# Attention, expert and softplus kernel: score products on keys laid out as block diagonals, scores issued ahead of the previous tile's turning, two score banks, another order of early loads

## The chip, the cores and the metric

The kernel runs on one core of a Trainium2 chip. The metric is device time of the whole program in microseconds (us); a run's time is that of one execution, and the median of several runs is compared. Five engines work side by side and meet through semaphores: TensorE (PE; its weight loads are shown apart as PEld), VectorE (DVE), ScalarE (ACT), GpSimd (POOL) and SyncE (SP), which here issues most transfers. Each engine takes its own instructions strictly in the order in which they are queued. PSUM has 8 banks of 128 x 512 fp32.

## The reference, cut to what matters

```python
def _attn_ref(q, k, v):                      # B, H, S, D = 4, 8, 576, 64
    scores = np.matmul(q, k.transpose(0, 1, 3, 2)) / np.sqrt(D)
    rel = pos[:, None] - pos[None, :]
    mask_plain = (rel >= 0) & (rel < 32)                      # heads 0 to 3
    mask_dil = (rel >= 0) & (rel < 128) & (rel % 4 == 0)      # heads 4 to 7
    scores = np.where(masks, scores, -1e9)
    attn = np.exp(scores - scores.max(-1, keepdims=True))
    attn = attn / (attn.sum(-1, keepdims=True) + 1e-09)
    return np.matmul(attn, v)

def reference(...):
    x = attn_out.transpose(0, 2, 1, 3).reshape(2304, 512)
    x = _moe_ref(x, ...)     # each token to the one of 8 experts with the largest logit
    return _moe2_ref(x, ...) # softplus(x @ w_in) @ w_out
```

## The kernel before, in words

**Stages.** The program is one long list written out by hand. First come 20 attention tiles (4 batches of 5; tile `w` of batch `b` covers 128 query positions, the last of a batch 64), mixed with the routing of tokens to experts. Then the eight experts ("ranks", the largest expert known first as rank 0) follow, and then the softplus part in blocks of 384 tokens. PE, ACT, DVE and SP take their instructions in the order of the Python text (`manual_schedule`, L1020); pools (`bufs`) decide when a buffer is free again.

**Keys and queries.** `load_qk` (L258) brings 576 KB of q or k of four heads into a `raw` tile; `transpose_qk` (L295) turns 512 columns at a time on PE into a PSUM tile `pqk`, and `evict_qk` (L287) copies from there into `qT` (scaled, L291 on DVE or L293 on ACT) or `kT` (L289 on ACT). There are ten such units a batch (`QK_UNITS`), of which eight are turned by L304 and two small ones, with the ninth piece of both q and k, by L314. In `qT` and `kT` the 64 dimensions of one head lie on partitions 0 to 63, those of the other head of a pair on 64 to 127. Units of the next batch are spread over the tiles of this one by `QK_0` and `QK_AT` (tile by tile, how many; `some_qk`). `load_v` (L266) fills `vP` (heads 0 to 3) and `vD` (heads 4 to 7); `fills` (L235) writes zeros with GpSimd into the parts of them that must be empty.

**One tile.** `scores` (L338) first writes the mask into two PSUM banks with two products against an identity (L346), then adds 32 products of 64 partitions, 32 queries and 64 (or 48) keys (L361), 16 for each half of the partitions, each half into its own bank. `softmax` (L371) takes the minimum of each 64 (the scores carry a minus sign; L376, result `mx`) and subtracts (L377, result `p`) on DVE; `exps` (L383) is one exponential on ACT in place. `transpose_p` (L387) turns `p` on PE (L391, result `pp`), `evict_p` copies it out on ACT (L400, `pt`). `values` (L403) are 16 products of 128 partitions, 32 queries and 128 columns (L418, result `o`); `sums` (L422) and `normalise` (L433) on DVE make the row sums (L426 to L430) and `x` (L440), which SP stores to DRAM (L447, L450). `transpose_x` turns x on PE (L457, `px`), `evict_x` copies it on ACT (L468, `xT`).

**Routing.** For each of six groups of tiles `logits_of` makes router products (L478, `pl`); the generators `logits`, `route` and `pick` add small DVE steps (`lt`, L494 and L497; turned on PE at L500; one-hot `roh`, L551; rank products on PE at L564 to L568). `pump` takes the next one or two of these steps at fixed places in a tile's text, so they stand between the softmax and normalising steps. `events` places single steps of the end by tile number: at tile 18 the first expert weights are split on ACT (L759, `wh`) and DVE (L704, `wl`).

**The order in a step.** The loop at L1101 runs `i` from 0 to 21. A step issues, in this order: turning and copying of p of tile i-1, scores of tile i, the step's turnings of q and k but one, turning of x of tile i-2, softmax and exponential of tile i, values, sums and normalising of tile i-1, the last turning of q and k. So the scores of a tile stand behind the turning of the previous tile's p on PE, and there is one pair of score banks (`ps_s`, `bufs=1`).

**Start.** SP's queue begins with q and k of batch 0, then v's plain half (`load_v(0, 0)`), q and k of batch 1's first half, v's dilated half (`load_v(0, 1)`); L1021 to L1033.

Of the kernel before, what the change touches and what calls it, by code (L numbers as in the profile page):

```python
# [40 lines left out]
def attn_moe_softplus_kernel(ctx: ExitStack, tc: tile.TileContext, q, k, v, w_gate, w_ogate, w1, w2, w_in, w_out, out, dbg=None):  # L41
# [177 lines left out]
    ps_s = psctx.enter_context(tc.tile_pool(name="ps_s", bufs=1, space=PSUM))  # L219
# [5 lines left out]

    SH = 8
    QS = S + 64 + SH
    qT = [per_p[i].tile([P, 2, 2, QS], F32, name=f"qT{i}") for i in range(2)]  # L230
    kT = [per_p[i].tile([P, 2, 2, S + SH], F32, name=f"kT{i}") for i in range(2)]
# [3 lines left out]
    def fills(i):  # L235


        for h2 in range(2):
            nc.gpsimd.memset(qT[i][64 * h2 : 64 * h2 + 64, 1, :, S + SH * h2 :], 0.0)
# [55 lines left out]
    def transpose_qk(b, half, ti, y):  # L295
# [3 lines left out]
        ps = ps_t.tile([P, 512], F32, tag="tp", name=f"pqk{b}{half}{ti}{y}")  # L299
        if y < 2:  # L300
# [4 lines left out]
            for o in range(2):  # L305
                src = ps[64 * o : 64 * o + 64].rearrange("q (j x p) -> q x p j", j=4, x=2)
                dst = (qT, kT)[ti][b % 2][64 * y : 64 * y + 64, half, :, SH * y : SH * y + S]
                dst = dst.rearrange("q x (p j) -> q x p j", j=9)[:, :, :, y + o : y + o + 7 : 2]
                evict_qk(b, half, ti, dst, src)
        else:  # L310
# [27 lines left out]
    def scores(b, w):  # L338

        i = b % 2  # L340
        s = ps_s.tile([P, 2, 512], F32, tag="s", name=f"s{b}{w}")
        mask = mask_w[:, 0:1].to_broadcast([P, 4, 64]) if w else mask_0.unsqueeze(2).to_broadcast([P, 2, 2, 64])
        for h2 in range(2):
            o = s[:, h2, :256]
            o = o.rearrange("q (c k) -> q c k", k=64) if w else o.rearrange("q (a c k) -> q a c k", a=2, k=64)
            nc.tensor.matmul(o, identb, mask, start=True, stop=False, skip_group_check=True)  # L346
        for half in range(2):
            nk = 64 if w < 4 or half == 0 else 48
            for hp in range(2):
                for u in range(4):  # L350
                    for h2 in range(2):
                        rows = slice(64 * h2, 64 * h2 + 64)
                        q_, k_ = [t[rows, half, hp, SH * h2 : SH * h2 + n_] for t, n_ in ((qT[i], S + 64), (kT[i], S))]
                        if half == 0:
                            n = 4 * w + (u if w < 4 else u % 2)
                            q0, k0 = 32 * n, 32 * max(n - 1, 0)
                        else:
                            q_, k_ = [t.rearrange("q (m r) -> q r m", r=4)[:, u] for t in (q_, k_)]
                            q0, k0 = 32 * w, 32 * max(w - 1, 0)
                        c = 64 * (2 * half + hp)  # L360
                        nc.tensor.matmul(  # L361
                            s[32 * u : 32 * u + 32, h2, c : c + nk],
                            q_[:, q0 : q0 + 32],
                            k_[:, k0 : k0 + nk],
                            start=False,
                            stop=(half == 1 and hp == 1 and u == 3),
                            skip_group_check=True,
                        )
        tl[b, w] = dict(s=s)

    def softmax(b, w):  # L371
        d = tl[b, w]
        mx = sm_p.tile([P, 2, 4], F32, tag="mx", name=f"mx{b}{w}")
        p = at_p.tile([P, 4, 2, 64], F32, tag="p", name=f"p{b}{w}")
        s = d["s"][:, :, :256].rearrange("q h (c k) -> q h c k", k=64)
        nc.vector.tensor_reduce(mx, s, AX.X, ALU.min)  # L376
        nc.vector.tensor_tensor(  # L377
            p.rearrange("q c h k -> q h c k"), mx.unsqueeze(3).to_broadcast([P, 2, 4, 64]), s, ALU.subtract
        )
        pump()  # L380
        d["p"] = p
# [513 lines left out]
    def acc(c):  # L895
        if ("a", c // 2) not in xacc:
            xacc["a", c // 2] = (ps_s, ps_o)[c // 2].tile([P, 2, 512], F32, tag="so"[c // 2], name=f"xacc{c}")
        xacc[c] = xacc["a", c // 2][:, c % 2]
# [127 lines left out]
    fills(0)  # L1026
    load_qk(1, 0)
    load_v(0, 1)
# [14 lines left out]
    QK_0 = [1, 2, 2, 2, 3]  # L1043
# [57 lines left out]
    for i in range(n + 2):  # L1101
# [13 lines left out]
        if 1 <= i < n + 1:  # L1115
            transpose_p(*tiles[i - 1])
            evict_p(*tiles[i - 1])
        if i < n:
# [12 lines left out]
            scores(b, w)  # L1131
        events(i, 0)
        some_qk(nqk - 1)
        if 2 <= i:
# [335 lines left out]
```

## Time and profile before

| what | us |
|---|---|
| median of 3 runs | 847.83 (847.11 to 848.87) |
| the profiled execution | 845.49 |
| its span, first to last instruction | 843.9 |
| attention tiles, first mask product to the end of the last scores | 15.1 to 148 |
| rest of routing, rank 0's tokens | to 179.8 |
| experts and softplus | 179.8 to 843.9 |
| PE busy over the span | 780.8 (93%) |
| DVE, ACT, POOL busy | 544.6, 470.6, 191.3 |

Times in the rows are us from the span's start, durations of one instruction ns where a "mean" stands. A group of instructions has one row: line, engine, operation, what is written and read, shape, count; then busy time and mean, and behind the second bar the time in which its engine sat idle just before it, with what ended most of that time ("issue": nothing that the profile shows). Products in fp32 leave two records each. PEclk is the mean granted share of TensorE's full clock.

### The profile page before, as it was taken

The page shows a single profiled execution, that of the slowest core. Times are in us where ns is not written, and L with a number is a line of the kernel's source. Part 1 is how long each engine was busy: PE and PEld are TensorE (multiplying, and loading weights), DVE is VectorE, ACT ScalarE, POOL GpSimd, SP SyncE. Part 2 cuts the span into 40 slices and gives each one's busy share as a digit, 9 for nine tenths or more (in the row PEclk, how much of TensorE's full clock was granted, in tenths as well). Part 3 has the DMA queues.
Part 4 walks back from the last instruction along what each step waited for, and adds up shares of the span by engine and source line. Part 5 has one row for each costly group of instructions (what it writes and reads, how often), then busy time and mean ns, then how long its engine had stood idle before and what let it go on. Part 6 is the DMA issues. An engine that isn't in the chain of part 4 may idle for free.

```text
span 843.9 us, 16072 instructions
## 1 busy us (share of the span) xinstructions
PE 780.8 (93%) x6202; PEld 705.4 (84%) x6203; DVE 544.6 (65%) x1074; ACT 470.6 (56%) x901; POOL 191.3 (23%) x171
## 2 busy tenths in 40 slices
PE   5788865799999999999799999999999999999995
PEld 4566644689899999999798888899999999999994
DVE  4467756473266767743679989886666665766653
ACT  3564533345456566655666666665655655655553
POOL 9101024325233533543201221211001001001001
PEclk8898989699999999999999999999999999999999
DMA  9959766317588889776841313231000001000000
GB/s 218 243 148 182 153 114 202 107 34 226 177 279 253 279 280 295 245 217 200 307 120 50 101 51 94 57 94 38 19 1 37 1 1 38 1 1 38 1 1 37
DMA packets 88850, 104.26 MB, mean 124 GB/s; under 512 B 31005, under 2 KB 65181, under 8 KB 88769
## 3 DMA queue, kind: packets, MB, share of 16 engines
q1 hardware_dynamic: 78688, 87.50, 37.5%
q0 software_dynamic: 3888, 10.12, 3.7%
q10 hardware_dynamic: 6192, 5.56, 2.0%
q8 instruction: 50, 0.82, 0.4%
q14 instruction: 32, 0.25, 0.1%
HBM read 83.98 MB, written 19.32 MB: 122 GB/s over the span
## 4 chain that ended last, share of the span: by engine, by line
PE 44%; issue 16%; DVE 7%; ACT 3%; POOL 1%; DMA 1%; SPq 0%; POOLq 0%; DVEq 0%
PE q L1379 4%; PE pg L843 4%; PE pg L844 4%; PE pg L842 4%; PE q L1377 4%; PE q L1378 4%; PE ph L842 3%; PE ph L844 3%; PE py L842 3%; PE ph L843 3%; PE py L843 3%; PE py L844 3%; DVE l L1357 1%; ACT gh L1363 1%; DVE l L1355 1%
## 5 line engine op out<-in xcount | busy, mean ns | idle before, releaser
L704 POOL TENSOR_TENSOR wl<-wr,wh 128x1024 fp32r<-128x1024 f32 (+1 forms) x46 | 98.2, 2144 | 207.6 <-ACT wh L788 108.2
L843 PE MATMUL pg<-xlm,wh 128*128 128x384 f32 x384 | 129.6, 338 | 0.0
L842 PE MATMUL pg<-xhm,wh 128*128 128x384 f32 x384 | 129.4, 337 | 0.0
L844 PE MATMUL pg<-xhm,wl 128*128 128x384 f32 x384 | 129.4, 337 | 0.0
L1379 PE MATMUL q<-wh,gl 128*128 128x512 f32 x288 | 114.1, 396 | 2.2 <-DVE gl L704 2.1
L1377 PE MATMUL q<-wh,gh 128*128 128x512 f32 x288 | 113.9, 396 | 0.5
L1378 PE MATMUL q<-wl,gh 128*128 128x512 f32 x288 | 113.0, 392 | 0.0
L1363 ACT CAST gh<-l 128x384 fp32r<-128x384 f32 x96 | 49.2, 512 | 99.7 <-DVE l L1357 99.7
L842 PE MATMUL ph<-xh,wh 128*128 128x424 f32 (+7 forms) x256 | 80.7, 315 | 3.9 <-DVE hl L856 2.3
L704 DVE TENSOR_TENSOR gl<-l,gh 128x384 fp32r<-128x384 f32 x96 | 57.1, 594 | 41.0 <-ACT gh L1363 38.1
L759 ACT CAST wh<-wr 128x1024 fp32r<-128x1024 f32 x72 | 75.2, 1048 | 14.5 <-ACT y L865 6.1
L843 PE MATMUL py<-hl,wh 128*128 128x424 f32 (+7 forms) x256 | 80.2, 313 | 2.4 <-DVE hl L856 2.4
L842 PE MATMUL py<-hh,wh 128*128 128x424 f32 (+7 forms) x256 | 81.3, 318 | 0.0
L1386 POOL DMA_INDIRECT out_dram<-o,perm_sb x18 | 18.6, 1034 | 271.9 <-DVE o L254 137.5
L844 PE MATMUL ph<-xh,wl 128*128 128x424 f32 (+7 forms) x256 | 80.1, 313 | 0.0
L844 PE MATMUL py<-hh,wl 128*128 128x424 f32 (+7 forms) x256 | 80.0, 312 | 0.0
L843 PE MATMUL ph<-xl,wh 128*128 128x424 f32 (+7 forms) x256 | 79.9, 312 | 0.0
L842 PEld LDWEIGHTS pg<-xhm,wh 128*128 128x128 f32 x384 | 72.1, 188 | 3.9
L843 PEld LDWEIGHTS pg<-xlm,wh 128*128 128x128 f32 x384 | 72.0, 188 | 3.9
L704 DVE TENSOR_TENSOR wl<-wr,wh 128x1024 fp32r<-128x1024 f32 x42 | 59.4, 1417 | 20.7 <-ACT wh L759 20.7
L844 PEld LDWEIGHTS pg<-xhm,wl 128*128 128x128 f32 x384 | 72.1, 188 | 0.0
L1348 DVE TENSOR_SCALAR w<-u 128x384 f32<-128x384 f32 x96 | 34.7, 361 | 56.5 <-ACT u L1346 55.7
(192 smaller groups left out, 1639.4 us busy)
## 6 DMA issues: line engine op xcount, KB each, us to landing
wr<-in_moe_w_dram SPq DMA_DIRECT2D x64, 512.0 KB
raw<-in_q_dram SPq DMA_DIRECT2D x8, 576.0 KB
raw<-in_k_dram SPq DMA_DIRECT2D x8, 576.0 KB
x2r<-yT_dram SPq DMA_DIRECT2D x12, 384.0 KB
vP<-in_v_dram SPq DMA_DIRECT2D x16, 272.0 KB
praw<-in_moe_w_in_dram SPq DMA_DIRECT2D x8, 512.0 KB
praw<-in_moe_w_out_dram SPq DMA_DIRECT2D x8, 512.0 KB
wr<-in_moe_w_in_dram SPq DMA_DIRECT2D x8, 512.0 KB
```

The lines of the kernel that those rows point to most:

```text
L704: e.tensor_tensor(lo, src, hi.bitcast(F32), ALU.subtract)
L759: (eng or nc.scalar.copy)(d[1], d[0])
L842: nc.tensor.matmul(ps, wh, xh, start=(first and i == 0), stop=False)
L843: nc.tensor.matmul(ps, wh, xl, start=False, stop=False)
L844: nc.tensor.matmul(ps, wl, xh, start=False, stop=(last and i == k - 1))
L1348: nc.vector.tensor_scalar(w_, u, 1.0, None, ALU.add)
L1355: nc.vector.tensor_tensor(l, l, w_, ALU.add)
L1363: nc.scalar.copy(gT[b, f][0], l)
L1377: nc.tensor.matmul(acc[b, t], gh[:, ts_], wh, start=(f == 0), stop=False)
L1378: nc.tensor.matmul(acc[b, t], gh[:, ts_], wl, start=False, stop=False)
L1379: nc.tensor.matmul(acc[b, t], gl[:, ts_], wh, start=False, stop=(f == NF - 1))
L1386: sc = nc.gpsimd.indirect_dma_start(out=out, out_offset=IndirectOffsetOnAxis(ap=perm_sb[:, b * (BT // P) + t, 0:1], axis=0), in_=o, in_off ...
```

## The change

What it does:

- **Keys as block diagonals.** `kT` gets one more dimension of two: for each half of the partitions only its own head's slot is filled and the other slot is zero (GpSimd, in `fills`). A product over all 128 partitions with two slots of 64 columns gives both heads' scores next to each other. `scores` issues 16 such products a tile and one mask product of 512 columns, all into one bank. The offset `SH` of the second head is gone, and with it the copies that covered all 128 partitions: the small copies of a pair (L317) are now made in two halves.
- **Two tiles' scores are held.** `ps_s` has two buffers of one bank.
- **Order in a step.** Scores and softmax come first, then turning and copying of p of the tile before; the exponential follows the first turnings of q and k; the sums of the tile before stand ahead of its values; one turning of q and k moves ahead of the values.
- **Early loads.** `load_v(0, 1)` goes ahead of `load_qk(1, 0)`; batch 1 is turned 0, 1, 3, 3, 3 units a tile (`QK_0`) in place of 1, 2, 2, 2, 3.
- **Buffers.** `p` and `pt` have two buffers in place of three, `x` five in place of six.

```diff
-    ps_s = psctx.enter_context(tc.tile_pool(name="ps_s", bufs=1, space=PSUM))
+    ps_s = psctx.enter_context(tc.tile_pool(name="ps_s", bufs=2, space=PSUM))
...
-    kT = [per_p[i].tile([P, 2, 2, S + SH], F32, name=f"kT{i}") for i in range(2)]
+    kT = [per_p[i].tile([P, 2, 2, 2, S], F32, name=f"kT{i}") for i in range(2)]
...
         for h2 in range(2):
-            nc.gpsimd.memset(qT[i][64 * h2 : 64 * h2 + 64, 1, :, S + SH * h2 :], 0.0)
+            nc.gpsimd.memset(kT[i][64 * h2 : 64 * h2 + 64, :, :, 1 - h2], 0.0)
+        nc.gpsimd.memset(qT[i][:, 1, :, S:], 0.0)
...
-            for t in range(2):
-                dst = (qT, kT)[t][b % 2][:, half, :, SH : SH + S].rearrange("q x (p j) -> q x p j", j=9)[:, :, :, 0]
-                evict_qk(b, half, t, dst, ps[:, P * t : P * t + P].rearrange("q (x p) -> q x p", x=2))
+            for y in range(2):
+                for t in range(2):
+                    src = ps[64 * y : 64 * y + 64, P * t : P * t + P].rearrange("q (x p) -> q x p", x=2)
+                    evict_qk(b, half, t, to(t, y)[:, :, :, 8 - 8 * y], src)
...
     def scores(b, w):
...
-        s = ps_s.tile([P, 2, 512], F32, tag="s", name=f"s{b}{w}")
...
-        for h2 in range(2):
-            o = s[:, h2, :256]
...
-            nc.tensor.matmul(o, identb, mask, start=True, stop=False, skip_group_check=True)
+        s = ps_s.tile([P, 512], F32, tag="s", name=f"s{b}{w}")
+        s4 = s.rearrange("q (c h k) -> q c h k", h=2, k=64)
...
+        nc.tensor.matmul(o, identb, mask, start=True, stop=False, skip_group_check=True)
...
-                    for h2 in range(2):
...
-                        nc.tensor.matmul(
-                            s[32 * u : 32 * u + 32, h2, c : c + nk],
-                            q_[:, q0 : q0 + 32],
-                            k_[:, k0 : k0 + nk],
...
+                    nc.tensor.matmul(
+                        s4[32 * u : 32 * u + 32, 2 * half + hp, :, :nk],
+                        qu[:, q0 : q0 + 32],
+                        ku[:, :, k0 : k0 + nk],
...
-        p = at_p.tile([P, 4, 2, 64], F32, tag="p", name=f"p{b}{w}")
+        p = at_p.tile([P, 4, 2, 64], F32, tag="p", name=f"p{b}{w}", bufs=2)
...
-        pt = at_p.tile([P, 4, P], F32, tag="pt", name=f"pt{b}{w}")
+        pt = at_p.tile([P, 4, P], F32, tag="pt", name=f"pt{b}{w}", bufs=2)
...
-        x = at_p.tile([P, 2, 4, D], F32, tag="x", name=f"x{b}{w}", bufs=6)
+        x = at_p.tile([P, 2, 4, D], F32, tag="x", name=f"x{b}{w}", bufs=5)
...
     load_v(0, 0)
     fills(0)
+    load_v(0, 1)
     load_qk(1, 0)
-    load_v(0, 1)
...
-    QK_0 = [1, 2, 2, 2, 3]
+    QK_0 = [0, 1, 3, 3, 3]
...
-        if 1 <= i < n + 1:
-            transpose_p(*tiles[i - 1])
-            evict_p(*tiles[i - 1])
...
             scores(b, w)
+            softmax(b, w)
+        if 1 <= i < n + 1:
+            transpose_p(*tiles[i - 1])
+            evict_p(*tiles[i - 1])
         events(i, 0)
         some_qk(nqk - 1)
+        if i < n:
+            exps(*tiles[i])
         if 2 <= i:
             transpose_x(*tiles[i - 2])
             evict_x(i - 2)
             pump()
         events(i, 1)
-        if i < n:
-            softmax(*tiles[i])
-            exps(*tiles[i])
+        if 1 <= i < n + 1:
+            sums(*tiles[i - 1])
         events(i, 2)
+        some_qk(min(nqk, 1))
         if 1 <= i < n + 1:
             values(*tiles[i - 1])
-            sums(*tiles[i - 1])
             normalise(*tiles[i - 1])
         events(i, 3)
-        some_qk(min(nqk, 1))
```

Three places in the queues show the move. A row names the line, the operation, what it writes and reads, and how many stand in a row; s is a tile's scores, pqk a turning of q or k, pp and px turnings of p and x, o the values (vP and vD the two halves of v). The weight load of the identity ahead of each mask product, and the second of two mask products alike, are not shown. PE's queue from the first tile's mask, before:

```order
L346 MATMUL s_327<-mask_86,identb 128x256
L361 MATMUL s_327<-kT_116,qT_114 32x64 x32
L304 MATMUL pqk_367<-identf,raw_222 128x128 x4
L391 MATMUL pp_374<-identf,p_363 128x128 x4
L346 MATMUL s_385<-mask_w,identb 128x256
L361 MATMUL s_385<-kT_116,qT_114 32x64 x32
L304 MATMUL pqk_420<-identf,raw_224 128x128 x4
L418 MATMUL o_432<-vP_118,pt_379 32x2x64 x8
L418 MATMUL o_432<-vD_120,pt_379 32x2x64 x8
```

and now:

```order
L346 MATMUL s_333<-mask_86,identb 128x512
L359 MATMUL s_333<-kT_116,qT_114 32x128 x16
L346 MATMUL s_360<-mask_w,identb 128x512
L359 MATMUL s_360<-kT_116,qT_114 32x128 x16
L388 MATMUL pp_382<-identf,p_352 128x128 x4
L306 MATMUL pqk_395<-identf,raw_231 128x128 x4
L415 MATMUL o_402<-vP_118,pt_387 32x2x64 x8
L415 MATMUL o_402<-vD_120,pt_387 32x2x64 x8
```

The scores of tiles 0 and 1 now run back to back and the turning of tile 0's p behind both; the first turning of batch 1's q has moved from ahead of that p to behind it, one step later; 32 products of 64 columns are 16 of 128.

PE's queue around the scores of tile 19, the last (px is tile 17's x and then tile 18's, pl the router products and plt the turning of the logits lt of one group of tiles), before:

```order
L457 MATMUL px_2374<-identf,x_2323 128x128 x4
L418 MATMUL o_2401<-vP_119,pt_2337 32x2x64 x8
L418 MATMUL o_2401<-vD_121,pt_2337 32x2x64 x8
L478 MATMUL pl_2425<-xT_2169,wg 32x128 x12
L500 MATMUL plt_2451<-identf,lt_2438 128x96
L391 MATMUL pp_2453<-identf,p_2387 128x128 x4
L346 MATMUL s_2460<-mask_w,identb 128x256
L361 MATMUL s_2460<-kT_117,qT_115 32x64 x16
L361 MATMUL s_2460<-kT_117,qT_115 32x48 x16
L457 MATMUL px_2495<-identf,x_2423 128x128 x4
```

and now:

```order
L454 MATMUL px_2074<-identf,x_2035 128x128 x4
L415 MATMUL o_2101<-vP_119,pt_2071 32x2x64 x8
L415 MATMUL o_2101<-vD_121,pt_2071 32x2x64 x8
L475 MATMUL pl_2125<-xT_1903,wg 32x128 x12
L346 MATMUL s_2146<-mask_w,identb 128x512
L359 MATMUL s_2146<-kT_117,qT_115 32x128 x8
L359 MATMUL s_2146<-kT_117,qT_115 32x2x48 x8
L497 MATMUL plt_2168<-identf,lt_2138 128x96
L388 MATMUL pp_2170<-identf,p_2063 128x128 x4
L454 MATMUL px_2178<-identf,x_2118 128x128 x4
```

Tile 19's mask and scores have moved ahead of the turnings of lt and of tile 18's p, behind which they stood.

DVE's queue around the softmax of tile 18 (mx, p: its minimum and subtraction; sm, rc, x: sums, reciprocals and normalised output of tiles 16 and 17; wl: the low part of expert weights, which reads ACT's wh), before:

```order
L440 TENSOR_TENSOR x_2323<-o_2301,rc_2319 128x512
L704 TENSOR_TENSOR wl_0_2381<-wr_0_2043,wh_0_2380 128x1024
L376 TENSOR_REDUCE mx_2386<-s_2339 128x8
L377 TENSOR_TENSOR p_2387<-mx_2386,s_2339 128x2x4x64
L426 TENSOR_REDUCE sm_2418<-p_2297 128x8
L427 TENSOR_SCALAR sm_2418<-sm_2418 128x8
L430 RECIPROCAL rc_2419<-sm_2418 128x2x2x2
L440 TENSOR_TENSOR x_2423<-o_2401,rc_2419 128x512
L494 COPY lt_2438<-pl_2425 96x128
```

and now:

```order
L437 TENSOR_TENSOR x_2035<-o_2018,rc_2014 128x512
L373 TENSOR_REDUCE mx_2062<-s_2044 128x8
L374 TENSOR_TENSOR p_2063<-mx_2062,s_2044 128x512
L701 TENSOR_TENSOR wl_0_2081<-wr_0_1776,wh_0_2080 128x1024
L423 TENSOR_REDUCE sm_2086<-p_1987 128x8
L424 TENSOR_SCALAR sm_2086<-sm_2086 128x8
L427 RECIPROCAL rc_2087<-sm_2086 128x2x2x2
L437 TENSOR_TENSOR x_2118<-o_2101,rc_2087 128x512
L491 COPY lt_2138<-pl_2125 96x128
```

Tile 18's minimum and subtraction have moved ahead of wl; the sums, x and lt of tile 17 stand behind it as before.

## Rows read from the trace of the kernel before

**Rows 1.** Windows: stretch, length, busy (count) of PE, PEld, DVE, ACT, POOL; PEclk, DMA, GB/s.

```profile
15.10:48.40 33.30, 22.28 (x528) 16.70 (x525) 17.00 (x33) 17.63 (x30) 9.22 (x13) 0.90 1.07 230
48.40:75.40 27.00, 24.75 (x639) 19.05 (x638) 20.81 (x55) 18.00 (x32) 0.73 (x1) 1.00 0.79 176
75.40:114.50 39.10, 30.16 (x606) 23.19 (x605) 23.64 (x78) 18.37 (x34) 8.91 (x10) 0.83 0.75 142
114.50:153.30 38.80, 25.42 (x598) 19.01 (x596) 23.06 (x73) 11.55 (x21) 10.05 (x11) 0.88 0.55 166
...
179.80:843.90 664.10, 646.58 (x3636) 599.51 (x3636) 440.72 (x774) 390.20 (x758) 138.64 (x85) 1.00 0.36 113
```

**Rows 2.** Groups of PE by shape, 15 to 180 us; last ACT's eviction of kT.

```profile
L361 PE MATMUL s<-kT,qT 64*32 64x64 f32 x1152 | 22.9, 262 | 7.7 <-issue 5.7 <-ACT kT L289 1.9
L304 PE MATMUL pqk<-identf,raw 128*128 128x128 f32 x97 | 18.0, 315 | 4.0 <-DMA raw<-in_q_dram 4.0
L418 PE MATMUL o<-vP,pt 128*32 128x128 f32 x320 | 15.4, 307 | 0.0
...
L391 PE MATMUL pp<-identf,p 128*128 128x128 f32 x80 | 14.1, 303 | 5.4 <-ACT p L385 4.6 <-issue 0.8
...
L361 PE MATMUL s<-kT,qT 64*32 64x48 f32 x128 | 5.3, 271 | 4.1 <-issue 4.1
...
L500 PE MATMUL plt<-identf,lt 96*128 96x96 f32 x4 | 1.2, 312 | 7.2 <-DVE x L440 4.8 <-DVE lt L497 2.4
...
L565 PE MATMUL prk<-roh,upper 128*128 128x24 bf16 x4 | 0.7, 175 | 3.3 <-DVE roh L551 1.8 <-DVE roh L554 1.5
...
L289 ACT COPY kT<-pqk 128x128 f32<-128x128 f32 x7 | 2.9, 411 | 6.7 <-DVE pk L639 3.6 <-DVE x L440 1.6 <-DVE qT L291 1.4
```

**Rows 3.** Timeline of PE, one step: start, duration, group [idle before it].

```profile
60.80 0.38 PE L346 MATMUL s<-mask_w,identb 128*128 128x256 bf16 x2
61.11 1.12 PE L361 MATMUL s<-kT,qT 64*32 64x64 f32 x64
62.16 0.44 PE L314 MATMUL pqk<-identf,raw 128*128 128x128 f32 x2
...
62.96 0.65 PE L418 MATMUL o<-vP,pt 128*32 128x128 f32 x16
...
63.98 0.66 PE L304 MATMUL pqk<-identf,raw 128*128 128x128 f32 x4
...
64.96 0.38 PE L346 MATMUL s<-mask_w,identb 128*128 128x256 bf16 x2
```

**Rows 4.** The page's instruction queue (packets, MB, share), and PE's timeline from 76.8 us.

```profile
q8 instruction: 50, 0.82, 0.4%
...
76.80 0.30 PE L361 MATMUL s<-kT,qT 64*32 64x64 f32 x4 [0.44 <-issue]
...
80.52 0.74 PE L361 MATMUL s<-kT,qT 64*32 64x64 f32 x25 [1.01 <-issue]
81.20 1.11 PE L304 MATMUL pqk<-identf,raw 128*128 128x128 f32 x4
```

**Rows 5.** Timeline, DVE and PE at tile 18.

```profile
138.98 1.23 DVE L704 TENSOR_TENSOR wl<-wr,wh 128x1024 fp32r<-128x1024 f32 x1 [2.78 <-ACT wh L759]
...
140.12 0.68 DVE L376 TENSOR_REDUCE mx<-s 128x8 f32<-128x512 f32 x1
...
143.92 0.40 PE L500 MATMUL plt<-identf,lt 96*128 96x96 f32 x1 [4.81 <-DVE x L440]
```

**Rows 6.** Timeline of PE, the start of batch 0.

```profile
21.95 1.09 PE L304 MATMUL pqk<-identf,raw 128*128 128x128 f32 x4 [4.00 <-DMA raw<-in_q_dram]
...
30.95 0.27 PE L346 MATMUL s<-mask_w,identb 128*128 128x256 bf16 x1
```

**Rows 7.** Timeline of SP's queue, v loads of batch 2 and the store behind them.

```profile
65.09 5.63 SPq L273 DMA_DIRECT2D vP<-in_v_dram  x4
...
78.71 0.37 SPq L447 DMA_DIRECT2D x_dram<-x  x1
```

More of the change, by code (lines that the diff above doesn't have):

```diff
@@ L299, in transpose_qk, with to @@
         ps = ps_t.tile([P, 512], F32, tag="tp", name=f"pqk{b}{half}{ti}{y}")
+        def to(t, y):
+            dst = qT[b % 2][64 * y : 64 * y + 64, half] if t == 0 else kT[b % 2][64 * y : 64 * y + 64, half, :, y]
+            return dst[:, :, :S].rearrange("q x (p j) -> q x p j", j=9)
         if y < 2:
@@ L306, in transpose_qk @@
                 src = ps[64 * o : 64 * o + 64].rearrange("q (j x p) -> q x p j", j=4, x=2)
-                dst = (qT, kT)[ti][b % 2][64 * y : 64 * y + 64, half, :, SH * y : SH * y + S]
-                dst = dst.rearrange("q x (p j) -> q x p j", j=9)[:, :, :, y + o : y + o + 7 : 2]
-                evict_qk(b, half, ti, dst, src)
+                evict_qk(b, half, ti, to(ti, y)[:, :, :, y + o : y + o + 7 : 2], src)
         else:
@@ L340, in scores @@
         i = b % 2
[L341 to L346 removed]
+        s = ps_s.tile([P, 512], F32, tag="s", name=f"s{b}{w}")
+        s4 = s.rearrange("q (c h k) -> q c h k", h=2, k=64)
+        mask = mask_w[:, 0:1].to_broadcast([P, 8, 64]) if w else mask_0.unsqueeze(2).to_broadcast([P, 2, 4, 64])
+        o = s.rearrange("q (c k) -> q c k", k=64) if w else s.rearrange("q (a c k) -> q a c k", a=2, k=64)
+        nc.tensor.matmul(o, identb, mask, start=True, stop=False, skip_group_check=True)
         for half in range(2):
@@ L349, in scores @@
             for hp in range(2):
+                q_, k_ = qT[i][:, half, hp], kT[i][:, half, hp]
                 for u in range(4):
-                    for h2 in range(2):
[L352 to L360, printed above, removed]
-                        nc.tensor.matmul(
-                            s[32 * u : 32 * u + 32, h2, c : c + nk],
-                            q_[:, q0 : q0 + 32],
-                            k_[:, k0 : k0 + nk],
[L365 to L368, printed above, removed]
@@ L369, in scores @@
-        tl[b, w] = dict(s=s)
+                    if half == 0:
+                        n = 4 * w + (u if w < 4 else u % 2)
+                        q0, k0, qu, ku = 32 * n, 32 * max(n - 1, 0), q_, k_
+                    else:
+                        q0, k0 = 32 * w, 32 * max(w - 1, 0)
+                        qu = q_.rearrange("q (m r) -> q r m", r=4)[:, u]
+                        ku = k_.rearrange("q h (m r) -> q h r m", r=4)[:, :, u]
+                    nc.tensor.matmul(
+                        s4[32 * u : 32 * u + 32, 2 * half + hp, :, :nk],
+                        qu[:, q0 : q0 + 32],
+                        ku[:, :, k0 : k0 + nk],
+                        start=False,
+                        stop=(half == 1 and hp == 1 and u == 3),
+                        skip_group_check=True,
+                    )
@@ L371, in softmax @@
+        tl[b, w] = dict(s=s4.rearrange("q c h k -> q (c h) k"))
     def softmax(b, w):
         d = tl[b, w]
-        mx = sm_p.tile([P, 2, 4], F32, tag="mx", name=f"mx{b}{w}")
-        p = at_p.tile([P, 4, 2, 64], F32, tag="p", name=f"p{b}{w}")
-        s = d["s"][:, :, :256].rearrange("q h (c k) -> q h c k", k=64)
-        nc.vector.tensor_reduce(mx, s, AX.X, ALU.min)
+        mx = sm_p.tile([P, 8], F32, tag="mx", name=f"mx{b}{w}")
+        p = at_p.tile([P, 4, 2, 64], F32, tag="p", name=f"p{b}{w}", bufs=2)
@@ L895, in acc @@
     def acc(c):
-        if ("a", c // 2) not in xacc:
-            xacc["a", c // 2] = (ps_s, ps_o)[c // 2].tile([P, 2, 512], F32, tag="so"[c // 2], name=f"xacc{c}")
-        xacc[c] = xacc["a", c // 2][:, c % 2]
+        if c < 2:
+            xacc[c] = ps_s.tile([P, 512], F32, tag="s", name=f"xacc{c}")
+        else:
+            if "a" not in xacc:
+                xacc["a"] = ps_o.tile([P, 2, 512], F32, tag="o", name=f"xacc{c}")
+            xacc[c] = xacc["a"][:, c % 2]
     def acc0(c):
```

6 lines of the change are left out of this document (3 added, 3 removed).

## The prediction

> **What bounds the kernel now.** I read the stages first [rows 1]. From 179.8 us on TensorE (PE) is busy for 646.58 of 664.10 us; none of its instructions there is touched, so that stretch only starts earlier or later. What the change can move lies before it. From 15.1 to 153.3 us the 20 attention tiles run, in four batches of five. In batch 1 (48.4 to 75.4) PE is busy for 24.75 of 27.00 us: it is the limit there, and 2.25 us is all that a better order can take. In batches 2 and 3 (75.4 to 153.3) it is busy for 55.58 of 77.90 us, at a mean granted clock of 0.83 and 0.88 (its levels are 1.2 and 2.4 GHz). DVE is nowhere full (23.64 of 39.10, 23.06 of 38.80).
>
> Then the idle time before PE's groups [rows 2]: 9.8 us before score products with no releaser seen ("issue": 5.7 and 4.1); 4.6 us before turning p (releaser: the exponential); 4.8 us once, and 2.4 in two pieces, before turning lt (releaser: DVE); 3.3 us before the rank products (roh, DVE); 4.0 us once for a q load. Third, one undisturbed step of TensorE [rows 3]: from one mask to the next 60.80 to 64.96, 4.16 us, where nothing waits.
>
> **The change, part by part.**
>
> *Block diagonals.* 32 products of 64 rows and 64 columns become 16 of 128 rows and 128 columns, and two mask products become one of double width. The score group takes 61.11 to 62.16, 1.05 us [rows 3]. The trace has the new shape already: the values are 16 products of 128*32 with 128x128, and take 62.96 to 63.98, 1.02 us [rows 2, 3]. The mask pair's 0.31 us (60.80 to 61.11) I set equal to one wide product. So 0, bounds 2 gained (0.1 a tile) and 1 lost. The Trainium skill ("TensorEngine Tiling (Array Packing)", Theoretical Speedup) speaks against the change: a contraction of 64 gains up to 2x from row tiling, which is given up here. The row of the values does not bear that out; what the rule would do is the third rival.
>
> *Fewer instructions.* From 15.1 to 153.3 us PE has 528+639+606+598 = 2371 product records [rows 1], of which 1152+128 = 1280 are scores [rows 2]. Half of these go: 640 of 2371, 27%. That matters if the issue time is the instruction stream coming late. It looks so: from 76.80 PE does four records at a time with gaps of 0.3 to 1 us, until 25 run at once at 80.52; a queue of kind "instruction" moves 50 packets and 0.82 MB, 16 KB each [rows 4]; and SP is just then issuing v loads (65.09, done before 78.71) [rows 7]. With 27% fewer records I take 27% of 9.8 us, 2.6 us; bounds 0 (each block that is left comes just as late) and 9.8. The Trainium skill ("Runtime: NRT & Kernel Launch", Instruction fetch mechanics) tells of blocks of 16 KiB with 256 instructions, which agrees with that size, but says that the fetch is hidden since dispatch is slower. By that rule this term and the next are 0 and the time would be 838.9; the gaps from 76.80 on say otherwise.
>
> *The clock behind a stall.* After the gap that ends at 80.52, four transposes take 1.11 us (81.20), against 0.66 at 63.98 [rows 3, 4]: the lower level. A stall that goes takes this along. Two long stalls with about 2 us each behind them, a quarter of it: 1 us; bounds 0 and 4.
>
> *Scores ahead of turning p.* Before, pp(i-1) stands ahead of scores(i), so scores wait for an exponential that itself waits for scores(i-1): one closed circle a step. Now scores(i) come first, into the second score bank, and the exponential of tile i-1 has a whole step. All 4.6 us go [rows 2]; bounds 2 and 4.6. With two p and pt buffers in place of three nothing new waits: subtraction i+2 follows the sums of tile i on DVE, and pt(i) follows values(i-2) on PE.
>
> *Tile 18.* DVE stood idle for 2.78 us, for ACT's cast wh, until it could do wl at 138.98, and that tile's maximum came behind it (140.12), then sums, x and lt, for which PE waited 4.81 us until 143.92 [rows 5]. Now tile 18's maximum and subtraction stand ahead of wl, and tile 19's scores ahead of lt's turning. I take 4 of 4.8 us, since wl still stands ahead of the sums of tile 17 and so of its x and lt; bounds 0 and 4.8.
>
> *Routing.* Turnings of lt and rank products now stand behind a score group too where they stood ahead of one, which gives DVE 1.36 us (60.80 to 62.16 [rows 3]) more. Of 2.4 + 3.3 us [rows 2] I take 2; bounds -3 and 5.7, since on DVE the softmax now goes ahead of route steps.
>
> *Early loads.* The second half of v is loaded ahead of batch 1's q and k, and batch 1's turnings start in step 1. Before, PE stood 4.00 us for that q until 21.95; tile 2's mask started at 30.95 [rows 6]. Now scores 0 and 1 run back to back, and q comes later by the v that goes first: 4 x 192 and 4 x 48 KB by the shapes, 0.98 MB, at 230 or 176 GB/s [rows 1] 4.3 to 5.6 us, so an estimate of 26.3 to 27.5. Behind it stand one turning (1.11 at the low level [rows 4]) and the values: tile 2's mask at about 29.5, 1.5 us earlier, but with two turnings of q and k fewer done (0.66 us each [rows 3]). And evictions that are now split by halves of the partitions cost ACT 0.41 us more for each kT one [rows 2], twice ahead of scores 0: 0.8 us. So 0; bounds 3 gained and 2 lost. Later ACT hides the small ones (18.00 of 27.00 busy [rows 1]).
>
> *kT's zero fill* on GpSimd: four more fills, beside loads; later nobody waits there (0.73 us busy from 48.4 to 75.4 [rows 1]). 0.
>
> *Given back.* DVE's softmax (0.68 at 140.12 [rows 5], and a subtraction as long) now runs ahead of sums and normalising, for which PE's turning of x waits; and in batch 1 there is only 2.25 us to win. I take 1.7 us, a little over a third of the circle's 4.6; bounds 0 and 8.
>
> Sum: 2.6 + 1 + 4.6 + 4 + 2 + 0 - 1.7 = 12.5 us. The profiled execution has a span of 843.9 and took 845.49, 1.6 around the span; the median of the runs is 847.83, 2.3 above it. So span 831.4, that execution 833.0, median 835.3.
>
> **The rivals.**
>
> *The stalls go with the stream* (0.17). If the blocks are only just late, more lead for each hides nearly all: the remaining 7.2 us of issue time and 3 us of low clock come on top, 835.3 - 10.2 = 825.1. For it: the gaps stand in score groups, whose records halve. Against: they coincide with v loads, which stay and now fall into a shorter time.
>
> *The circle was not the limit* (0.17). Scores come earlier, but PE is busy anyway (batch 1), or waits where p's waits stood for x, lt and rank products; the stalls stay. Of 12.5 some 4 are left: 843.8. Then the second score bank does not do what it is for. For it: 24.75 of 27.00 [rows 1].
>
> *Row packing lost, slower* (0.09). The two halves of the array ran side by side; if 16 full products stream twice as long, scores take 2.10 us in place of 1.05: 20 x 1.05 = 21 us on PE, less 12.5: 856.3. It decides from 12.5/20 = 0.63 us more a tile, scores above 1.68 us. Against: the values' 1.02 us.
>
> *Five x buffers* (0.02) make it slower only if a store lands later than five steps: the store of tile 6's x, whose values end by 63.98 [rows 3], was issued at 78.71 behind v's loads, 14.7 us later [rows 7]; five steps at 4.16 us [rows 3] are 20.8, so this decides only where steps are shorter than about 3 us or the store takes over 6 us to land.
>
> **How the numbers follow.** The forecast has 0.55. The range runs from 823 to 846: below it lies the lower half of the first rival (0.08), above it the slower ones and a little of the second (0.12). About 0.2% (1.7 us) is what can be told from no change. Faster: 0.55 + 0.17 + 0.11 of the second = 0.83; same: 0.05, of the second; slower: 0.12.
>
> **What would show it.** Right: turning p never waits for an exponential; a score group of 32 records lasts 1.0 to 1.1 us; no wait of over 1 us for lt behind tile 18; fewer and shorter issue gaps; the first rank 0 products start near 167 in place of 179.8 and the rest keeps its 664 us. Wrong: score groups of 1.7 us; waits for x, lt and rank products of 8 us; gaps of 4 us still standing behind v loads; DVE waiting for x's stores.

## The result, and the profile after

The changed kernel takes 837.83 us (median of 17 runs), the kernel before 846.09 beside it (17 runs): a ratio of 0.9906, 95% interval 0.9886 to 0.9927, or 8 us. A second comparison (f1_changed_again) gave 0.9917 (0.9892 to 0.9942). The forecast was 12.5 us. The profiled execution's span fell from 843.9 to 837.5, 6.4 us.

The windows of the changed kernel, cut at the same masks as [rows 1] (stretch, length, busy and count of PE, PEld, DVE, ACT, POOL, then PEclk, DMA share, GB/s):

```profile
15.70:45.90 30.20, 22.88 (x359) 16.10 (x357) 16.39 (x31) 17.17 (x31) 16.23 (x24) 0.89 1.10 238
45.90:73.80 27.90, 25.36 (x445) 18.57 (x440) 21.09 (x55) 18.75 (x35) 0.00 (x0) 1.00 0.79 180
73.80:108.50 34.70, 27.57 (x474) 20.09 (x470) 24.70 (x84) 18.80 (x38) 6.34 (x7) 1.00 0.82 146
108.50:146.90 38.40, 27.95 (x435) 19.48 (x429) 23.32 (x71) 12.95 (x25) 10.71 (x12) 0.87 0.54 146
...
173.40:837.50 664.10, 648.56 (x3636) 600.99 (x3636) 443.14 (x774) 390.50 (x759) 140.72 (x86) 0.99 0.36 113
```

Against [rows 1]: the last stage keeps its 664.1 us and starts 6.4 earlier. Batch 0 is 3.1 us shorter, batch 2 4.4, batch 3 0.4; batch 1, where PE was full, is 0.9 **longer**, with 0.6 us more of PE busy. The windows do not hold quite the same work: 32 records of router products, 1.6 us, have moved from batch 1's window to batch 2's (64 and 24 records before, 32 and 56 now), so batch 1 lost more than 0.9 and batch 2 gained more than 4.4. Batch 2 has the full clock now (1.00 after 0.83).

The groups of PE by shape in the same stretch (columns as in [rows 2]):

```profile
L359 PE MATMUL s<-kT,qT 128*32 128x128 f32 x576 | 31.3, 338 | 9.7 <-issue 4.8 <-ACT kT L286 4.8
L415 PE MATMUL o<-vP,pt 128*32 128x128 f32 x320 | 15.1, 298 | 3.2 <-ACT pt L397 3.2
L306 PE MATMUL pqk<-identf,raw 128*128 128x128 f32 x96 | 14.9, 282 | 7.4 <-DMA raw<-in_q_dram 5.2 <-PE px L454 1.1 <-ACT kT L286 0.9
...
L388 PE MATMUL pp<-identf,p 128*128 128x128 f32 x80 | 13.5, 292 | 0.4 <-ACT p L382 0.4
L454 PE MATMUL px<-identf,x 128*128 128x128 f32 x80 | 13.3, 290 | 4.3 <-DVE x L437 3.7 <-ACT kT L286 0.3 <-DMA vD<-in_v_dram 0.2
L475 PE MATMUL pl<-xT,wg 128*32 128x128 f32 x160 | 11.5, 304 | 3.9 <-ACT xT L465 3.9
...
L359 PE MATMUL s<-kT,qT 128*32 128x96 f32 x64 | 3.5, 349 | 0.0
...
L314 PE MATMUL pqk<-identf,raw 128*128 128x128 f32 x14 | 2.8, 284 | 1.9 <-DVE rpm L576 1.3 <-ACT kT L286 0.6
...
L497 PE MATMUL plt<-identf,lt 96*128 96x96 f32 x4 | 1.2, 297 | 1.6 <-DVE lt L494 1.6
```

The waits for the exponential are gone (0.4 after 4.6), gaps without a releaser halved (scores 4.8 after 9.8), and lt's wait is 1.6 after 7.2. New are 3.2 us for pt and 1.3 for rpm; grown are those for kT before scores (4.8 after 1.9), for q, x and xT. And the score group is not 1.05 us long. One step of PE, as in [rows 3]:

```profile
54.55 0.39 PE L346 MATMUL s<-mask_w,identb 128*128 128x512 bf16 x1
54.87 1.56 PE L359 MATMUL s<-kT,qT 128*32 128x128 f32 x32
56.36 0.66 PE L388 MATMUL pp<-identf,p 128*128 128x128 f32 x4
...
58.26 0.65 PE L415 MATMUL o<-vP,pt 128*32 128x128 f32 x16
58.72 0.62 PE L415 MATMUL o<-vD,pt 128*32 128x128 f32 x16
59.27 0.33 PE L497 MATMUL plt<-identf,lt 128*128 128x128 f32 x1
59.43 0.38 PE L346 MATMUL s<-mask_w,identb 128*128 128x512 bf16 x1
```

The scores take 54.87 to 56.36, 1.49 us; the values, as many records of the same shape, 58.26 to 59.27, 1.01. So 0.44 us were lost in a tile that nothing disturbs, 8.8 us if all 20 lose as much, and still the kernel is faster. The score groups' own busy time rose by less, 6.6 us (22.9 + 5.3 [rows 2] to 31.3 + 3.5): records that come late one by one count as busy for longer, and before there were more of these. In batches 0 and 1 it rose by 2.3 us each (5.55 to 7.81, 5.46 to 7.80), in batch 3 by 2.7 (7.50 to 10.17), and in batch 2 it fell by 0.6 (8.89 to 8.28).

### The profile page after: what moved, and what is told of

It reads as the page before. It is cut to its first block, busy times and chain, and to the rows that moved or that the text cites. A ratio compares the mean times of both kernels' runs of the same rounds, so it can differ in the third digit from the quotient of the medians.

```text
span 837.5 us, 14769 instructions
## 1 busy us (share of the span) xinstructions
PE 784.0 (94%) x5542; PEld 701.9 (84%) x5543; DVE 551.9 (66%) x1079; ACT 473.7 (57%) x912; POOL 199.7 (24%) x173
## 4 chain that ended last, share of the span: by engine, by line
PE 46%; issue 16%; DVE 6%; ACT 3%; POOL 1%; DMA 1%; SPq 0%; POOLq 0%; DVEq 0%
PE q L1380 4%; PE pg L840 4%; PE pg L841 4%; PE pg L839 4%; PE q L1378 4%; PE q L1379 4%; PE ph L839 3%; PE ph L841 3%; PE ph L840 3%; PE py L839 3%; PE py L840 3%; PE py L841 3%; DVE l L1358 1%; DVE gl L701 1%; ACT gh L1364 1%
## 5 line engine op out<-in xcount | busy, mean ns | idle before, releaser
L701 DVE TENSOR_TENSOR wl<-wr,wh 128x1024 fp32r<-128x1024 f32 x42 | 61.9, 1478 | 20.4 <-ACT wh L756 14.1
```

The source lines that it names most:

```text
L701: e.tensor_tensor(lo, src, hi.bitcast(F32), ALU.subtract)
```

## The experiments

"Issue time" is the sum, over PE's groups from 15 us to the first rank product, of idle time without a releaser, in the one profiled execution of each kernel: 12.7 us before, 5.0 in the changed kernel (5.6 in its second profile). The ratios and their intervals are those on record; they are not the quotients of the two medians (839.88 over 845.83 is 0.9930, the ratio of that kernel 0.9961).

### The change taken apart

**e1_rowpacked**: the changed kernel with the score products, key layout and copies of before, and one pair of score banks.

```diff
-    ps_s = psctx.enter_context(tc.tile_pool(name="ps_s", bufs=2, space=PSUM))
+    ps_s = psctx.enter_context(tc.tile_pool(name="ps_s", bufs=1, space=PSUM))
...
-    kT = [per_p[i].tile([P, 2, 2, 2, S], F32, name=f"kT{i}") for i in range(2)]
+    kT = [per_p[i].tile([P, 2, 2, S + SH], F32, name=f"kT{i}") for i in range(2)]
...
```

> The changed kernel with the score products of before: 32 products of 64 rows in two banks, keys without the zero slots, one pair of score banks; order in a step, early loads and buffers as changed. Theory: the block diagonals cost PE 1.50 us a tile in place of 1.05 (31 records that start from 54.87 to 56.36 against 55.98 to 57.00), 20 x 0.45 = 9 us, and the gain of the change comes from order and loads in spite of it; a second score bank is not needed, since the subtraction of the tile before is long done. Then this kernel runs 7 to 9 us faster than the changed one, about 829 to 831, 0.980 of before. Rival: the fewer PE records are what helped, since the stalls without a releaser fell from 9.8 to 4.8 us before scores; then the stalls come back here, eat 5 us or more of the 9, and the time is 834 to 838. Second rival: one pair of score banks holds PE up behind DVE's subtraction; then PE shows waits for p of line 374 or so, and the time is above 838.

Measured: 839.88 us (10 runs) against 845.83 of before on the same chip, 0.9961 (0.9924 to 0.9998). By the ratios it is not faster than the changed kernel. The theory's number fell; the time is a little above the first rival's, and the second rival's wait is there too, once. The groups of PE in its profile:

```profile
L361 PE MATMUL s<-kT,qT 64*32 64x64 f32 x1152 | 23.9, 265 | 11.0 <-issue 7.5 <-ACT kT L289 3.5
...
L346 PE MATMUL s<-mask_w,identb 128*128 128x256 bf16 x32 | 6.5, 287 | 1.7 <-DVE p L377 1.7
```

The products are short again (23.9 us with 1152 records against 31.3 with 576), but issue time is 9.7 us, and the mean granted clock of the run 0.971 (0.981 in the changed kernel). The second score bank saves at most 1.7 us: that is all the waiting for a subtraction there is without it, once, at tile 1. In e4_order_alone below, which has one pair of banks and the old loads, there is none.

**e2_diagonals**: the kernel before with the block diagonals and their banks, copies and buffers; order and loads as before (the diff of the change without its last two parts).

> The kernel before with block diagonals alone (16 products, one bank a tile, two score buffers, small evictions in halves, two p and pt and five x buffers for room); order in a step and early loads as before. Theory: 9 us more for scores on PE, less the stalls that go with half of the records (5 us or so by the changed kernel's trace): 1 to 7 us slower than before, 847 to 853, ratio 1.001 to 1.008. Rival (records are what counts, the product's time is hidden in waits): 3 to 6 us faster, ratio 0.993 to 0.997.

Measured: 840.74 us (10 runs), 0.9965 (0.9935 to 0.9996). The rival held: faster, by an interval that ends just below 1, although its scores too take 1.5 us a tile. Its groups:

```profile
L359 PE MATMUL s<-kT,qT 128*32 128x128 f32 x576 | 31.9, 353 | 3.3 <-ACT kT L286 2.7 <-issue 0.3
...
L388 PE MATMUL pp<-identf,p 128*128 128x128 f32 x80 | 14.9, 316 | 8.1 <-ACT p L382 7.5 <-issue 0.6
```

Issue time is 3.7 us after 12.7; the closed circle of scores and exponential stands (7.5 us).

**e3_old_loads**: the changed kernel, early loads as before.

```diff
     fills(0)
-    load_v(0, 1)
     load_qk(1, 0)
+    load_v(0, 1)
-    QK_0 = [0, 1, 3, 3, 3]
+    QK_0 = [1, 2, 2, 2, 3]
```

> The changed kernel with the early loads and the spread of batch 1's turnings as before. The prediction put this part at 0, bounds 3 gained and 2 lost. Theory: the new order of loads cost 1.2 us of waiting for q (5.21 in place of 4.00) and saved the wait for v; the mask of tile 2 starts at 30.29 in place of 30.95; so about even: 836 to 840. Rival: with scores 0 and 1 back to back the old loads would have let PE go on earlier, and this kernel is 2 to 4 us faster than the changed one, 834 to 836.

Measured: 835.94 us (4 runs), 0.9892 (0.9818 to 0.9966). By the ratios it is 1 to 2 us better than the changed kernel, which the intervals do not separate. In its profile PE waits 2.1 us for q (5.2 with the new loads), and the first rank product stands at 170.56, 2.9 us earlier. The wait for q varies with the old loads too: 4.0 before, 4.5 in e4_order_alone, 1.4 in e2_diagonals.

**e4_order_alone**: the kernel before with the new order in a step (and the smaller p, pt and x).

> The kernel before with the new order in a step alone (and the smaller p, pt and x buffers): 32 row-packed products, one pair of score banks, loads as before. Theory: order carries the gain, circle of p, tile 18 and routing, 10.6 us by the prediction's terms less 1.7: ratio 0.987 to 0.990, 835 to 838, about as good as the whole change. Rival: without the second score bank or the fewer records the order brings little, ratio 0.995 to 1.0.

Measured: 839.03 us (10 runs), 0.9920 (0.9885 to 0.9956); the theory's range was missed by a little, the rival's by more, and the interval reaches into both. By the medians the order alone brings most of the gain. No wait for an exponential is left, but

```profile
L361 PE MATMUL s<-kT,qT 64*32 64x64 f32 x1120 | 23.5, 263 | 11.6 <-issue 8.6 <-ACT kT L289 2.9
L418 PE MATMUL o<-vD,pt 128*32 128x128 f32 x320 | 15.5, 293 | 3.0 <-issue 2.0 <-DMA vD<-in_v_dram 1.0
```

issue time is 13.0 us. So e4_order_alone and e3_old_loads, on one chip and apart only in the diagonals with their second bank, differ by 13.0 to 5.6 us of issue time and by 839.03 to 835.94. So the 7.4 us saved there, with the clock behind them, paid for the longer products; whether 3 us more came of it, the intervals (0.9885 to 0.9956 and 0.9818 to 0.9966) do not say.

### What the products cost

**e5_keys_in_a_row**: the changed kernel, reading other keys for heads 4 to 7.

```diff
-                        ku = k_.rearrange("q h (m r) -> q h r m", r=4)[:, :, u]
+                        ku = k_[:, :, S // 4 * u : S // 4 * (u + 1)]
```

> The changed kernel, but the products of heads 4 to 7 read 64 keys that lie next to each other in place of every fourth one (so these heads' scores are of the wrong keys). In the changed kernel the 16 records of heads 0 to 3 take 0.46 us and the 16 of heads 4 to 7 take 1.03. Theory: it is the step of four elements that halves the rate; then a tile's scores take 0.95 in place of 1.50 us, PE has 20 x 0.5 = 10 us less to do, of which batch 1, where PE is full, gets all and the others half: 829 to 833, 0.980 to 0.985 of before. Rival: the slow records come from the second half's order or bank, or PE waits elsewhere for what it saves: 836 to 839.

Measured: the scores send tokens to other experts, so that all behind the attention is 86 us longer and the whole time, 915.94 us (1.0933 of before), says nothing. Its step of PE does:

```profile
53.64 0.39 PE L346 MATMUL s<-mask_w,identb 128*128 128x512 bf16 x1
53.96 1.08 PE L359 MATMUL s<-kT,qT 128*32 128x128 f32 x32
54.97 0.66 PE L388 MATMUL pp<-identf,p 128*128 128x128 f32 x4
...
58.04 0.38 PE L346 MATMUL s<-mask_w,identb 128*128 128x512 bf16 x1
```

Scores take 1.01 us (53.96 to 54.97) after 1.49, with nothing else changed: it is the step of four elements in the streamed keys. Half of 1.01 is taken for the half without that step; so the half with it takes 1.49 - 0.5 = 0.99, twice as long.

**e6_without_late_v** and **e7_rowpacked_without_late_v**: the changed kernel, and e1_rowpacked, without v of batches 2 and 3.

```diff
-                if w == 2:
+                if w == 2 and b == 0:
                     for half in range(2):
                         load_v(b + 1, half)
```

> The changed kernel without the loads of v for batches 2 and 3 (those batches use the values of batches 0 and 1). Theory: PE's gaps without a releaser are blocks of its instructions that stand behind the small packets of v (from 100 to 105 us 2904 packets, nearly all of 256 B, and more than the 16 engines' time); then the 4 us of gaps from 111 to 116 go, and the low clock from 123 with them: issue time under 1 us from 70 us on, 830 to 834. Rival: the blocks come late whatever else is loaded; the gaps stay at 4 to 5 us and the time within 2 us of the changed kernel's.

> The kernel with the row-packed products and the new order (e1_rowpacked) without the loads of v for batches 2 and 3, as in e6_without_late_v. Theory: row packing is worth 0.45 us a tile, and e1_rowpacked gave that back in stalls of its longer instruction stream (9.7 us without a releaser against 5.0); with the small packets gone the stalls fall to under 3 us, and this kernel is 4 to 9 us faster than e6_without_late_v: 822 to 829. Rival: the longer stream stalls without v's packets too (over 6 us), and the two are equal within 2 us.

Measured, on one chip: 828.53 us (0.9862, 0.9816 to 0.9908) and 823.12 us (0.9798, 0.9752 to 0.9844), 4 runs each. Issue time is 0.2 and 5.2 us. So the longer stream stalls without v's packets too, and still the row-packed kernel is 5.4 us faster by medians. How much of that the products bring is not shown: the two profiles are 4.0 us apart, of which 1.3 lie before the first rank product (157.61 against 158.89), 0.8 of them ahead of the first mask; the rest is behind it, where the kernels are the same. One undisturbed step, with the same work in both, gives the price of the diagonals cleanly; first e6, then e7, from mask to mask:

```profile
53.63 0.39 PE L346 MATMUL s<-mask_w,identb 128*128 128x512 bf16 x1
53.95 1.57 PE L359 MATMUL s<-kT,qT 128*32 128x128 f32 x32
...
58.53 0.38 PE L346 MATMUL s<-mask_w,identb 128*128 128x512 bf16 x1
```

```profile
51.38 0.39 PE L346 MATMUL s<-mask_w,identb 128*128 128x256 bf16 x2
51.70 1.10 PE L361 MATMUL s<-kT,qT 64*32 64x64 f32 x64
...
55.80 0.38 PE L346 MATMUL s<-mask_w,identb 128*128 128x256 bf16 x2
```

4.90 us against 4.42: 0.48 us a tile. What e6 does not show is that v's packets make the stalls. e5_keys_in_a_row and the next kernel ran on the same chip with all of v and have 0.2 us of issue time as well. On that chip the kernel before took 837.5 us (12 runs), 8 less than on the others.

**e8_keys_dealt_out**: the diagonals with keys of heads 4 to 7 stored by residue, so that the right keys lie in a row.

```diff
-            src = t[b, 4 * half : 4 * half + 4].rearrange("(y x) (p j) d -> (x p) y (j d)", x=2, j=9)
+            n_, j_ = (96, 12) if half and ti else (P, 9)
+            src = t[b, 4 * half : 4 * half + 4].rearrange("(y x) (p j) d -> (x p) y (j d)", x=2, j=j_)
...
+        def deal(y, o, j, n, c):
+            src = ps[64 * o : 64 * o + 64, c : c + 192 * n].rearrange("q (j r p) -> q p j r", r=2, p=96)
+            dst = kD[b % 2][64 * y : 64 * y + 64, y].rearrange("q r x m -> q r (x m)").rearrange("q r (p j) -> q r p j", j=3)
+            evict_qk(b, half, 1, dst[:, o::2, :, j : j + n].rearrange("q r p j -> q p j r"), src)
...
-                        ku = k_.rearrange("q h (m r) -> q h r m", r=4)[:, :, u]
+                        ku = kD[i][:, :, u, hp]
```

> The changed kernel with the keys of heads 4 to 7 stored by residue modulo 4, so that the products of e5_keys_in_a_row read the right keys: k of these heads is loaded as 96 partitions of 12 tokens, turned in twelve products of 96 columns in place of nine of 128, and copied out by residue (six small copies a batch in place of four). Theory: as e5_keys_in_a_row, less 1 to 2 us for three more products and the small copies a batch: 830 to 835. Rival: the copies with a step in both inner dimensions cost ACT more than PE saves, and q and k units come late: 838 or more.

Measured: 834.46 us (9 runs, 830.73 to 839.78), 0.9981 (0.9943 to 1.0018) of a kernel before that took 837.5 there. The mechanism works,

```profile
54.10 0.39 PE L373 MATMUL s<-mask_w,identb 128*128 128x512 bf16 x1
54.42 1.08 PE L386 MATMUL s<-kT,qT 128*32 128x128 f32 x32
...
58.50 0.38 PE L373 MATMUL s<-mask_w,identb 128*128 128x512 bf16 x1
```

and the step is 4.40 us, as short as the row-packed one. But waits for kT before scores are 7.1 us (6.1 and 6.5 in e5 and e6 on this chip), and no gain over the changed kernel can be claimed: that one did not run on this chip. Where the rest of the 0.4 us a tile went is open.

### Trying for a better version

**f1_changed_again** is the changed kernel, as the measure for three more on one chip.

> The changed kernel itself once more, as the measure for the other three, since chips differ by more than the terms in question (before had a median of 845.8 us beside the first four experiments and of 837.5 beside the second four). Expected 0.986 to 0.994 of before, as in the first comparison (0.9906).

Measured: 838.00 us (6 runs) against 844.65 of before, 0.9917 (0.9892 to 0.9942), as expected.

**f2_late_v_spread**, and the same edit in e4_order_alone (**f3_order_spread**) and in e8_keys_dealt_out with the early loads of before (**f4_dealt_spread**):

```diff
-    def load_v(b, half):
+    def load_v(b, half, heads=range(4)):
...
-        for h in range(4):
+        for h in heads:
...
-                if w == 2:
-                    for half in range(2):
-                        load_v(b + 1, half)
+                if w:
+                    load_v(b + 1, (w - 1) // 2, (2 * ((w - 1) % 2), 2 * ((w - 1) % 2) + 1))
```

> The changed kernel with the 12 transfers of the next batch's v issued over four steps (two heads of a half a step, steps 1 to 4 of a batch) in place of all in step 2. Nothing else differs. Theory: PE's gaps without a releaser are instruction blocks that stand behind v's small packets, so with these spread the gaps from 70 us on fall from 4.8 to under 1.5 us and the clock with them: 2 to 5 us faster than f1_changed_again. Rival: the same packets make the same delay in other places, or v comes late: within 1.5 us of it, or slower.

> e4_order_alone (row-packed products of before, new order in a step, early loads of before) with v's transfers spread over four steps as in f2_late_v_spread. Theory: e4_order_alone lost 13.8 us in gaps without a releaser and had 0.45 us a tile less of products; with the gaps under 6 us it beats the changed kernel by 3 to 7 us. Rival: the longer instruction stream stalls all the same (gaps over 9 us): equal to the changed kernel within 2 us.

> The changed kernel with the keys of heads 4 to 7 dealt out as in e8_keys_dealt_out, the early loads of before (e3_old_loads) and v's transfers spread (f2_late_v_spread). Theory: scores of 1.05 us a tile, half of the score records, few stalls: 7 to 13 us faster than f1_changed_again. Rival: e8_keys_dealt_out came out at 0.998 of before although its profile shows scores of 1.08 us; if the copies of k hold the tiles up (7.1 us of waiting for them there), this kernel is no faster than f1_changed_again.

Measured, 12 runs each: 841.40 us (0.9955, 0.9929 to 0.9980), 843.89 (0.9982, 0.9955 to 1.0010) and 846.77 (1.0018, 0.9998 to 1.0038). All three expectations of a gain fell. Issue time is 5.3, 11.1 and 5.4 us: it goes with the number of records, not with where v's transfers stand. And v came late, here in f2 (PE's timeline) and f4 (its group), both in the slowest of the 12 executions, 6 and 3 us above their medians:

```profile
93.86 1.08 PE L415 MATMUL o<-vD,pt 128*32 128x128 f32 x16 [5.08 <-DMA vD<-in_v_dram]
```

```profile
L442 PE MATMUL o<-vD,pt 128*32 128x128 f32 x320 | 15.1, 289 | 10.6 <-DMA vD<-in_v_dram 9.2 <-issue 1.4
```

## Why the prediction was right in sign, and which terms were off

The measured 8 us is two thirds of the forecast 12.5, and lies in the range. By terms of the sum:

- **Block diagonals, 0 (bounds 2 gained, 1 lost): 8.8 us lost** by the undisturbed step, 6.6 by the groups' busy time. This is the step that failed. I took the values' 1.02 us as the price of 16 full products; the values read columns that lie in a row, and half of the score products read every fourth key, a step written in the code. The rival "row packing lost" was a real mechanism, at 0.44 to 0.48 us a tile in place of the 1.05 it was priced at, below the 0.63 from which it would have decided. The Trainium skill ("TensorEngine Tiling (Array Packing)", Theoretical Speedup) puts row tiling of a contraction of 64 at up to 2x. I wrote that the row of the values did not bear that out; e5 and e7 do: 16 full products on keys in a row (1.01 us) only equal the 32 packed ones although half of those still read every fourth key (1.05). Where both read half of the keys at that step, packing gains 1.4 times (1.49 against 1.05), not 2; what the step costs the packed products no run shows.
- **Fewer instructions, 2.6 (bounds 0 and 9.8): 7.7 us** in the trace (12.7 to 5.0). The share was mis-sized, since I let stalls shrink only as the records do, by 27%. With the same chip and order, 13.0 fell to 5.6 and 5.2 to 0.2; likewise, across chips, 12.7 to 3.7 with the old order (before and e2) and 9.7 to 5.0 with the new (e1 and the changed kernel): halving the score records takes about half of it or more. Longer products are not what hides the gaps, since e5 and e8 have the short score time of e7 and 0.2 us. The rival "stalls go with the stream" was nearer here.
- **The clock, 1 (bounds 0 and 4): about 3.5 us in one batch.** Batch 2 went from a granted clock of 0.83 to 1.00. Without scores (8.89 us, now 8.28) and router products (1.05, now 2.53), which differ, PE's busy time there fell from 20.22 to 16.76 us; 32 records of turnings of q and k (L304, now L306), the same in both, from 6.6 to 5.1. Batch 0 and 3 kept their clock (0.90 to 0.89, 0.88 to 0.87).
- **Scores ahead of turning p, 4.6: 4.2** (4.6 to 0.4), as forecast. e4_order_alone shows it without the diagonals and with one pair of score banks, so the second bank, which I took as its means, is not needed for it.
- **Tile 18, 4: 1.4.** The wait for lt fell from 4.81 to 1.03 us, but PE now waits 2.36 us for pt ahead of it:

```profile
132.67 0.66 PE L388 MATMUL pp<-identf,p 128*128 128x128 f32 x4
...
135.49 0.58 ACT L397 COPY pt<-pp 128x512 f32<-128x512 f32 x1 [4.33 <-remote]
...
136.12 0.78 PE L415 MATMUL o<-vP,pt 128*32 128x128 f32 x16 [2.36 <-ACT pt L397]
```

  PE ended p's turning at 133.33 and ACT began to copy it 2.16 us later, with a releaser that the profile calls remote; DVE's minimum of tile 18 (135.37) waited the same way. Why is open, but the record shows where such waits stand. Two others of the changed kernel, before x, end at 85.87 and 115.76, 0.07 and 0.16 us after a gap of PE without a releaser; two more stand behind PE's waits of 2.42 and 1.31 us for x (150.39, 158.20). In e5 to e8, on the chip with the few gaps, neither DVE nor ACT has one. So these 6.1 us of PE's waiting may be the same stalls under another name; no run separates them.
- **Routing, 2: 2.8** (lt's other waits and roh's, 5.7, became 0.6 and 1.0, and 1.3 for rpm is new).
- **Early loads, 0 (bounds 3 gained, 2 lost): a little lost, if anything.** Two pairs of kernels that differ in it (e3 and the changed kernel, e4 and e1) say so with one sign (0.9892 to 0.9906 and 0.9920 to 0.9961), within their intervals. The forecast had q at 26.3 to 27.5 (it came at 27.40, with a wait of 5.21 us) and tile 2's mask at 29.5 (30.29).
- **Small copies: 0.8 at the start, 0 later.** The first mask came 0.67 us later, as forecast. But "later ACT hides them" failed: scores of a batch's first tile stand closer behind the last copies now, and PE waits 1.77 and 1.51 us for kT in batches 1 and 2 (0.57 and nothing before). The order alone (e4) makes it 0.62 and 0.88; the other 1.8 us came with the diagonals and their split copies.
- **Given back, 1.7 (bounds 0 and 8).** Waits that grew or are new, but for those named above: xT 1.4, x 1.0, px ahead of q's turnings 1.1, kT ahead of turnings and the rest of pt 2.3: 5.8 us. That the softmax ahead of sums and normalising is the cause, as I argued, is not shown: before x's 3.7 us DVE itself waited for a releaser that the profile calls remote.

From the first mask to the rank products PE's idle time fell from 40.6 to 32.9 us (164.70 - 124.11 and 157.70 - 124.77, lengths less busy time of the windows), while its busy time rose by 0.7: score products took 6.6 us more, and the turnings of q, k, p and x, the same work in both, 4.8 less (49.3 to 44.5 by their groups). That, and the start 0.6 us later, makes the 6.4 us of the profile. That the sum came out within a third is partly luck: the largest term had been put at nothing, and stalls and clock gave more than forecast.

Of the signs named, turning p hardly waits (0.4 us in all) and the rest kept its 664 us; scores of 1.0 to 1.1 us and a first rank product near 167 (it came at 173.5) failed. The rival that the circle was not the limit had 843.8 us, 0.995 of before; the intervals of the changed kernel (to 0.9927 and 0.9942) exclude that, though waits for x, xT and pt did grow, as it said. Five x buffers cost little that is seen: DVE waited 0.5 us for a store of x, 2.3 before.

## What to carry to other kernels

Price a new product by a row that has its shape *and* its access pattern: the count and shape of the values' products were right and the step of the streamed operand was not. Where PE's idle time has no releaser and shrinks with the number of records, the length of its instruction stream is itself a cost, paid twice when the clock drops behind a stall, so that a layout with longer products and half as many of them can come out even. And take the parts of a change apart before crediting one: here the order in a step brings 0.992 alone, the diagonals alone 0.9965, and the early loads nothing that the intervals show.

## What of the hardware was not expected

- Sixteen products of 128 columns took 1.01 us with keys in a row and 1.49 with half of them read at a step of four fp32 elements; the second half alone, by that sum, went from 0.5 to 0.99.
- Idle time without a releaser differs by chip: with 16 score products a tile 5.0 and 5.6 us in the changed kernel and 5.6 in e3_old_loads, but 0.2 in e5, e6 and e8 on a chip on which the kernel before took 837.5 us, not 846; with 32, 12.7 before and 13.0 in e4_order_alone, but 5.2 in e7 there (which lacks the late v). The page's instruction queue moves 50 packets with 32 score products a tile and 45 with 16 (0.82 and 0.74 MB). The Trainium skill ("Runtime: NRT & Kernel Launch", Instruction fetch mechanics) has the fetch hidden behind dispatch; the pairs above speak against that here, in that the gaps go with the number of records, though what delays a block stays open. A gap of the changed kernel, one record at a time:

```profile
110.64 0.27 PE L359 MATMUL s<-kT,qT 128*32 128x128 f32 x1 [1.13 <-issue]
111.39 0.28 PE L359 MATMUL s<-kT,qT 128*32 128x128 f32 x1 [0.48 <-issue]
112.78 0.41 PE L359 MATMUL s<-kT,qT 128*32 128x128 f32 x1 [1.12 <-issue]
```
